# Attention and two expert layers in one kernel: the second batch's keys and values loaded earlier, split with GpSimd, and the dispatch table cleared later

## The chip, the cores and the metric

The kernel runs on one core of a Trainium2 chip. The metric is device time in microseconds (us) of one execution; the runs before the change have a median of 566.87 us (3 runs, 565.37 to 568.51).

## The reference, cut to what matters

```python
# attention: batch 2, heads 8, sequence 576, head size 64
scores = q @ k.T / sqrt(64)
scores = where(scores >= max(scores) - tau, scores, -1e9)
x = (softmax(scores) @ v)                # as 1152 tokens x 512
# dense layer, 512 -> 2048 -> 512
x = elu(x @ w_in) @ w_out
# 8 experts, each token to one of them, at most 288 tokens an expert
e = argmax(x @ w_gate); p = softmax(x @ w_gate)[e]
disp[e, position of the token in e] = x  # slots that no token takes stay zero
out[token] = p * (relu(disp[e] @ w1[e]) @ w2[e])[position]
```

## The kernel before, in words

All matrix work is done in fp16 pairs: a float is split into a high half (the float, scaled and rounded) and a low half (what the rounding left), and three products of halves are summed. A split costs ScalarE the high half and a second engine the low half: VectorE with one instruction on the unscaled float, or GpSimd with a subtraction, for which ScalarE first scales the float in place. `split` (L101) has both forms, "dve" and "pool".

**Steps.** The attention loop (L903) runs 36 steps and two more for what lags. A step i is one tile of 128 query rows (i // 4) and one pair of heads (i % 4). Tiles 0 to 3 belong to the first batch, tile 4 to both, tiles 5 to 8 to the second, so the second batch's keys are first read for step 16's scores, which are issued at the end of step 15, and its values two steps after the scores. One step does, in order:

- PE: the product of probabilities and values of step i - 2 (`emit_pv`, L308);
- SyncE: loads of keys, values and queries (L198 to L211) into `kraw` and `qraw`, which share a ring of two buffers, and `vraw`, with two of its own;
- the splits of keys and values: the first half of each (`prep_k`, `prep_v`, L213 and L224: generators that stop after ScalarE's part);
- VectorE's row maximum (L274), ScalarE's exp (L284) for two heads;
- the second halves of the splits, on VectorE (L219, L229);
- in steps 0 to 16 a conversion of dense-layer weights (`conv`, L363; two a step from step 2 on): three VectorE instructions into one PSUM bank (L369 to L373), two on ScalarE that read it (L380, L381), one on GpSimd (L382), and the load of the weights four conversions ahead (`cst`);
- VectorE's mask (L290), and PE's scores of step i + 1 (L255), which take the PSUM that the mask has read;
- the split of the probabilities (L299 on ScalarE, L300 on GpSimd) and their DMA transpose on SyncE's queue (`pt`, L305);
- from step 7 on chunks of the dense layer, 48 matmuls of the first half (`mma`, L397) or 12 of the second (`mmb`, L429), with their own work on ScalarE (L411, L412, L418), VectorE (L414) and GpSimd (L419);
- every fourth step the attention output (L335 to L346) and the query split (`prep_q`, L234).

Each engine takes its instructions in the order in which the code writes them; SyncE's queue issues DMAs in that order too, and one that waits holds up those behind it. The loop's tables `CONV` and `FILL` say how many conversions and chunks a step has.

**The dispatch table.** `disp` in DRAM has 8 x 288 rows of 2,056 bytes (x in two halves, the gate weight and the token's number). `zero_fill` (L177) clears it in six parts at the ends of steps 8 to 13; `zeroed` then lets `route` (L514) write tokens into it by indirect DMA (L509). The experts read slots 0 to 207 of each expert (`load_x`, L650); slots from 196 on are read only where an expert has more than 196 tokens.

Of the kernel before, what the change touches and what calls it, by code (L numbers as in the profile page):

```python
# [7 lines left out]
F16 = mybir.dt.float16  # L8
# [33 lines left out]
def kernel(  # L42
# [126 lines left out]
    def setup_rest():  # L169
        nc.scalar.activation(out=wg[:, 0], in_=wg_f, func=ACTF.Copy, scale=SC)  # L170
        nc.vector.scalar_tensor_tensor(
            out=wg[:, 1], in0=wg_f, scalar=SC, in1=wg[:, 0], op0=ALU.mult, op1=ALU.subtract
        )
        nc.vector.tensor_copy(ev, ev_i)
        nc.vector.tensor_scalar(ids, ids, OOB_ID, None, ALU.bitwise_xor)

    def zero_fill(part, parts):  # L177
        n = E * CS // P
        r0, r1 = part * n // parts, (part + 1) * n // parts
        if r0 < r1:  # L180
            nc.sync.dma_start(
                out=disp.rearrange("(p r) (a c) -> p (r a) c", p=P, a=2)[:, 2 * r0:2 * r1],
                in_=zero.bitcast(U16).unsqueeze(1).to_broadcast([P, 2 * (r1 - r0), ROW // 2]),
            )
# [27 lines left out]

    def prep_k(b, j):  # L213
        k2 = raw_t.pop(("k", b, j))
        kt = attn.tile([P, 2, S], F16, name="kst", tag="kst", bufs=6)
        flat = kt.rearrange("p h s -> p (h s)")
        nc.scalar.activation(out=flat[0:D], in_=k2, func=ACTF.Copy, scale=SC)
        yield
        nc.vector.scalar_tensor_tensor(  # L219
            out=flat[D:P], in0=k2, scalar=SC, in1=flat[0:D], op0=ALU.mult, op1=ALU.subtract  # L220
        )
        kst[b, j] = kt

    def prep_v(b, j):  # L224
        v1 = raw_t.pop(("v", b, j))
        vt = attn.tile([P, 2, VC], F16, name="vst", tag="vst", bufs=6)
        nc.scalar.activation(out=vt[:, 0], in_=v1, func=ACTF.Copy, scale=SC)
        yield
        nc.vector.scalar_tensor_tensor(  # L229
            out=vt[:, 1], in0=v1, scalar=SC, in1=vt[:, 0], op0=ALU.mult, op1=ALU.subtract  # L230
        )
        vst[b, j] = vt

# [651 lines left out]
    with tc.manual_schedule():  # L885
        setup_first()
        setup_pool()
        for c in "kqgkcvcvcc":
# [8 lines left out]
            else:  # L897
                load_conv(len(stage_t))
        for _ in prep_k(0, 0):
            pass  # L900
        prep_q(0)
        sc = [emit_s(0, z) for z in range(2)]
        for i in range(NSTEP + LAG):  # L903
# [13 lines left out]
            halves = []  # L917
            for b, base in ((0, 0), (1, 4 * NPAIR)):
                jk = i + 1 - base
                if 0 <= jk + 1 < NPAIR and (b or jk >= 1):  # L920
                    load_k(b, jk + 1)
                if 0 <= jk < NPAIR:
                    halves.append(prep_k(b, jk))
                jv = i - base
                if 0 <= jv < NPAIR:
                    halves.append(prep_v(b, jv))
                if 0 <= jv + 1 < NPAIR and (b or jv >= 1):
                    load_v(b, jv + 1)
            if on and j == 0 and t_ + 1 < NTILE:
# [219 lines left out]
```

## Time and profile before

| | us |
|---|---|
| runs before: median, lowest, highest | 566.87, 565.37, 568.51 |
| profiled execution, its own time | 572.67 |
| its span, first to last instruction | 570.6 |
| busy: PE, DVE (VectorE), ACT (ScalarE), POOL (GpSimd) | 438.8, 400.1, 351.1, 266.8 |
| bytes moved by DMA | 105.59 MB, mean 185 GB/s |

The profile is of one execution, taken by the hardware profiler. Busy shares are means over a program with very different stages: attention with the dense layer between its steps (its last step begins at 326 us), the rest of the dense layer and the routing, then the experts. A row that says what an instruction waited for names the one that came last.

### The profile page before, as it was taken

What the parts mean: (1) busy time and instruction counts of PE and PEld (TensorE: products, weight loads), DVE (VectorE), ACT (ScalarE), POOL (GpSimd) and SP (SyncE); (2) the same over time, 40 slices, a digit from 0 to 9 for tenths busy, and PEclk for the clock granted to TensorE, in tenths of its full rate; (3) what the DMA queues carried; (4) which work ended last, traced back from release to release, by engine and by line L of the source; (5) the groups of instructions that cost most, each with busy time, mean ns of one, the idle gap of its engine ahead of it and who ended that gap; (6) DMA issues with size and microseconds to landing.
All of it is one profiled execution on the core that took longest, in us unless ns stands there. A gap on an engine that the chain in (4) does not pass through costs nothing.

```text
span 570.6 us, 13138 instructions
## 1 busy us (share of the span) xinstructions
PE 438.8 (77%) x5343; PEld 360.5 (63%) x5343; DVE 400.1 (70%) x840; ACT 351.1 (62%) x511; POOL 266.8 (47%) x195
## 2 busy tenths in 40 slices
PE   1143439575628889999999999998899997887792
PEld 0032327264506667777777777778799997887771
DVE  4888999998539879888887945765355676646620
ACT  3556577687437875865676756664386665756421
POOL 1236566767505544846656634232442442443232
PEclk9975668978868999999999999997899999799797
DMA  5864988999995556657976765755388989797521
GB/s 165 249 175 116 260 186 232 239 251 255 221 254 138 122 108 141 121 125 113 260 169 86 129 113 187 262 218 186 59 233 254 291 225 259 241 283 201 172 61 40
DMA packets 154227, 105.59 MB, mean 185 GB/s; under 512 B 135209, under 2 KB 142121, under 8 KB 150064
## 3 DMA queue, kind: packets, MB, share of 16 engines
q1 hardware_dynamic: 151520, 99.94, 70.9%
q0 software_dynamic: 2640, 4.74, 2.4%
q8 instruction: 44, 0.72, 0.5%
q14 instruction: 23, 0.19, 0.1%
HBM read 60.06 MB, written 12.68 MB: 127 GB/s over the span
## 4 chain that ended last, share of the span: by engine, by line
PE 26%; DMA 26%; DVE 25%; ACT 10%; issue 9%; POOL 2%; SPq 1%; POOLq 0%; DVEq 0%; ACTq 0%
PE mma L397 9%; DMA stg<-in_w_dram 9%; PE mmb L429 6%; DMA out_dram<-y,ix 5%; DMA kraw<-in_kt_dram 4%; DVE pp L290 4%; PE s L255 3%; DVE we L645 3%; ACT we L642 3%; DVE cvp L370 3%; PE pv L322 3%; DVE m L274 3%; DMA yr<-yt 3%; DVE cvp L369 3%; PE mm L682 2%
## 5 line engine op out<-in xcount | busy, mean ns | idle before, releaser
L255 PE MATMUL s<-kst,qst 128*128 128x288 f16 (+1 forms) x320 | 54.8, 338 | 82.4 <-DVE pp L290 72.6
L300 POOL TENSOR_TENSOR phl<-pp,phl 128x1152 f16<-128x1152 f32 x36 | 85.4, 2373 | 63.1 <-issue 45.1
L397 PEld LDWEIGHTS <-wi 128*128 128x128 f16 x1728 | 103.1, 100 | 4.5 <-issue 1.5
L645 DVE SCALAR_TENSOR_TENSOR we<-stg,we 128x1024 f16<-128x1024 f32 x64 | 79.2, 1274 | 37.2 <-ACT we L642 37.0
L255 PEld LDWEIGHTS <-qst 128*128 128x128 f16 (+1 forms) x320 | 30.3, 114 | 104.4 <-DVE pp L290 50.7
L642 ACT ACTIVATE we<-stg 128x1024 f16<-128x1024 f32 x64 | 64.3, 1047 | 44.0 <-DMA stg<-in_w_dram 43.3
L429 PE MATMUL mmb<-wo,g 128*128 128x512 f16 x384 | 89.7, 382 | 1.9 <-POOL g L419 1.8
L397 PE MATMUL mma<-xt,wi 128*128 128x128 f16 x1392 | 87.0, 225 | 0.5 <-DVE gf L414 0.5
L682 PE MATMUL mm<-xs,we 128*128 128x196 f16 x768 | 72.9, 259 | 13.4 <-DVE we L645 4.6
L682 PEld LDWEIGHTS <-we 128*128 128x128 f16 x768 | 69.4, 103 | 15.9 <-DVE we L645 9.6
L284 ACT ACTIVATE pp<-s,nb,escale 128x576 f32<-128x576 f32 x72 | 58.4, 827 | 24.7 <-DVE nb L275 10.4
L695 POOL TENSOR_TENSOR ht<-rf,ht 128x392 f16<-128x392 f32 x32 | 35.1, 1106 | 77.0 <-ACT ht L694 39.2
L429 PEld LDWEIGHTS <-g 128*128 128x128 f16 x384 | 35.4, 98 | 41.1 <-POOL g L419 3.4
L419 POOL TENSOR_TENSOR g<-gf,g 128x512 f16<-128x512 f32 x36 | 45.3, 1259 | 34.3 <-ACT g L418 34.3
L738 PE MATMUL mm<-ht,we 128*128 128x196 f16 x672 | 57.9, 247 | 1.5 <-DVE yt L749 1.5
L738 PEld LDWEIGHTS <-we 128*128 128x128 f16 x672 | 56.9, 97 | 1.6 <-issue 1.6
L290 DVE SCALAR_TENSOR_TENSOR pp<-s,th,pp 128x576 f32<-128x576 f32 x72 | 55.8, 812 | 2.1 <-ACT pp L284 1.9
L322 PE MATMUL pv<-vst,pt 128*128 128x64 f16 (+3 forms) x1080 | 46.0, 206 | 14.2 <-DMA pt<-phl 12.4
L274 DVE TENSOR_REDUCE m<-s 128x1 f32<-128x576 f32 x72 | 53.8, 748 | 2.1 <-PE s L255 2.1
L322 PEld LDWEIGHTS <-pt 128*128 128x128 f16 (+1 forms) x1080 | 43.6, 107 | 17.2 <-DMA pt<-phl 14.0
L299 ACT ACTIVATE phl<-pp 128x1152 f16<-128x1152 f32 x36 | 41.6, 1156 | 9.5 <-DVE pp L290 9.4
L382 POOL TENSOR_TENSOR wi<-cv,wi 128x512 f16<-128x512 f32 x16 | 18.5, 1155 | 46.5 <-ACT cv L381 46.5
(128 smaller groups left out, 619.5 us busy)
## 6 DMA issues: line engine op xcount, KB each, us to landing
stg<-in_w_dram SPq DMA_DIRECT2D x32, 1024.0 KB, 5.5
cst<-in_w_in_dram SPq DMA_DIRECT2D x16, 512.0 KB, 7.0
cst<-in_w_out_dram SPq DMA_DIRECT2D x16, 512.0 KB, 4.7
disp<-zero SPq DMA_DIRECT2D x6, 771.0 KB, 8.0
qraw<-in_qt_dram SPq DMA_DIRECT2D x9, 512.0 KB, 4.7
vraw<-in_vb_dram SPq DMA_DIRECT2D x8, 320.0 KB, 4.2
kraw<-in_kt_dram SPq DMA_DIRECT2D x8, 288.0 KB, 5.5
out_dram<-zero SPq DMA_DIRECT2D x1, 2304.0 KB, 9.2
```

Source lines behind the costliest of these rows:

```text
L255: nc.tensor.matmul(s[a:z, half, 0:288], q2[:, pas, h, a:z], kst[b, h // 2][:, h % 2, half * 288:(half + 1) * 288], start=(pas == 0), stop= ...
L274: nc.vector.tensor_reduce(out=m, in_=s, axis=AX.XY, op=ALU.max)
L284: nc.scalar.activation(out=pp[:, z].rearrange("p (a c) -> p a c", a=2), in_=s, func=ACTF.Exp, bias=nb, scale=escale,)
L290: nc.vector.scalar_tensor_tensor(out=e, in0=s, scalar=th, in1=e, op0=ALU.is_ge, op1=ALU.mult, accum_out=rsum[t_][:, h:h + 1],)
L300: nc.gpsimd.tensor_tensor(out=d[:, 1], in0=flat, in1=d[:, 0], op=ALU.subtract)
L322: nc.tensor.matmul(o[a:e, h:h + w // D, :].rearrange("p h d -> p (h d)"), q[:, ph * 9 + blk, a:e], vt[:, vh, c:c + w], start=(blk == 4 and ...
L397: nc.tensor.matmul(ps[:, o * P:(o + 1) * P], w[:, wh, kk, :], xt[t_][:, xh * 4 + kk, :], start=(k_ == 0), stop=(k_ == 11),)
L429: nc.tensor.matmul(ps, gt[t_, q][:, gh, o, :], w[:, wh, :], start=(first and o == 0 and n == 0), stop=(last_ and o == QF - 1 and n == 2),)
L642: nc.scalar.activation(out=w[:, 0, part], in_=t[:, part], func=ACTF.Copy, scale=SC)
L645: nc.vector.scalar_tensor_tensor(out=w[:, 1, part], in0=t[:, part], scalar=SC, in1=w[:, 0, part], op0=ALU.mult, op1=ALU.subtract)
L682: nc.tensor.matmul(ps[:, o * n:(o + 1) * n], w[:, wh, kk % 2, f * P:(f + 1) * P], t[:, xh * 4 + kk, :], start=(k_ == 0), stop=(k_ == 11),)
L738: nc.tensor.matmul(ps[:, o * n:(o + 1) * n], w[:, wh, f % 4, j * P:(j + 1) * P], h2[:, gh, f, :], start=(f == 0 and n_ == 0), stop=(f == 7 ...
```

## The change: what it does

- The loads and splits of keys and values follow four tables by step. For the second batch the four key loads move from steps 14 to 17 to steps 9, 11, 14 and 15, their splits from steps 15 to 18 to steps 12, 13, 16 and 17; the value loads from steps 15 to 18 to 12, 13, 16 and 18, their splits from steps 16 to 19 to 14, 15, 19 and 20. The first batch keeps its steps.
- Each split but the very first one of keys takes the form "pool": ScalarE scales in place and copies, GpSimd subtracts. `setup_rest` does the same with the gate weights `wg`.
- The clearing moves to steps 16 to 19, two experts a step, and covers slots 0 to 207 of each expert alone; in step 20 one small DMA clears the last 8 bytes of the rows from slot 208 on.

```diff
@@ -67,7 +67,12 @@
-    ZSTEP, ZPARTS, ZOUT = 8, 6, 26
+    ZIDS, ZSLOTS, ZOUT = 20, 16, 26
+
+    KLOAD = {0: (0, 2), 1: (0, 3), 9: (1, 0), 11: (1, 1), 14: (1, 2), 15: (1, 3)}
+    KPREP = {0: (0, 1), 1: (0, 2), 2: (0, 3), 12: (1, 0), 13: (1, 1), 16: (1, 2), 17: (1, 3)}
+    VLOAD = {1: (0, 2), 2: (0, 3), 12: (1, 0), 13: (1, 1), 16: (1, 2), 18: (1, 3)}
+    VPREP = {0: (0, 0), 1: (0, 1), 2: (0, 2), 3: (0, 3), 14: (1, 0), 15: (1, 1), 19: (1, 2), 20: (1, 3)}
@@ -167,20 +172,26 @@
-        nc.scalar.activation(out=wg[:, 0], in_=wg_f, func=ACTF.Copy, scale=SC)
-        nc.vector.scalar_tensor_tensor(
-            out=wg[:, 1], in0=wg_f, scalar=SC, in1=wg[:, 0], op0=ALU.mult, op1=ALU.subtract
-        )
+        split(wg[:, 0], wg[:, 1], wg_f, SC, "pool")
...
-    def zero_fill(part, parts):
-        n = E * CS // P
-        r0, r1 = part * n // parts, (part + 1) * n // parts
-        if r0 < r1:
+
+    CREAD = min(CS, -(-CMAIN // 16) * 16)
+
+    def zero_slots(e):
+        nc.sync.dma_start(
+            out=disp[e * CS:e * CS + CREAD].rearrange("(p r) (a c) -> p (r a) c", r=2, a=2),
+            in_=zero.bitcast(U16)[0:CREAD // 2].unsqueeze(1).to_broadcast([CREAD // 2, 4, ROW // 2]),
+        )
+
+    def zero_ids():
+
+        for a in range(CREAD, CS, P):
+            m = min(P, CS - a)
             nc.sync.dma_start(
-                out=disp.rearrange("(p r) (a c) -> p (r a) c", p=P, a=2)[:, 2 * r0:2 * r1],
-                in_=zero.bitcast(U16).unsqueeze(1).to_broadcast([P, 2 * (r1 - r0), ROW // 2]),
+                out=disp.rearrange("(e s) c -> s e c", e=E)[a:a + m, :, 2 * DM:],
+                in_=zero.bitcast(U16)[0:m, 0:4].unsqueeze(1).to_broadcast([m, E, 4]),
             )
@@ -210,26 +221,29 @@
-    def prep_k(b, j):
+    def prep(hi, lo, src, where):
+        if where == "pool":
+            nc.scalar.activation(out=src, in_=src, func=ACTF.Copy, scale=SC)
+            nc.scalar.activation(out=hi, in_=src, func=ACTF.Copy)
+            yield
+            nc.gpsimd.tensor_tensor(out=lo, in0=src, in1=hi, op=ALU.subtract)
+        else:
...
+    def prep_k(b, j, where="pool"):
         k2 = raw_t.pop(("k", b, j))
-        kt = attn.tile([P, 2, S], F16, name="kst", tag="kst", bufs=6)
+        kst[b, j] = kt = attn.tile([P, 2, S], F16, name="kst", tag="kst", bufs=6)
         flat = kt.rearrange("p h s -> p (h s)")
...
+        return prep(flat[0:D], flat[D:P], k2, where)
...
@@ -915,17 +929,14 @@
-            for b, base in ((0, 0), (1, 4 * NPAIR)):
-                jk = i + 1 - base
-                if 0 <= jk + 1 < NPAIR and (b or jk >= 1):
-                    load_k(b, jk + 1)
-                if 0 <= jk < NPAIR:
-                    halves.append(prep_k(b, jk))
-                jv = i - base
-                if 0 <= jv < NPAIR:
-                    halves.append(prep_v(b, jv))
-                if 0 <= jv + 1 < NPAIR and (b or jv >= 1):
-                    load_v(b, jv + 1)
+            if i in KPREP:
+                halves.append(prep_k(*KPREP[i]))
+            if i in VPREP:
+                halves.append(prep_v(*VPREP[i]))
+            if i in KLOAD:
+                load_k(*KLOAD[i])
+            if i in VLOAD:
+                load_v(*VLOAD[i])
@@ -965,9 +976,12 @@
-            if ZSTEP <= i < ZSTEP + ZPARTS:
-                zero_fill(i - ZSTEP, ZPARTS)
-                zeroed[0] = i == ZSTEP + ZPARTS - 1
+            if ZSLOTS <= i < ZSLOTS + E // 2:
+                for e in range(2):
+                    zero_slots(2 * (i - ZSLOTS) + e)
+            if i == ZIDS:
+                zero_ids()
+                zeroed[0] = True
```

From the attention code on, the changed kernel's lines stand some 14 higher: its L288 is L274 of before, L298 is L284, L319 is L305, L374 is L360.

How it moves instructions. SyncE's queue before, from the last zero transfer, at the end of step 13, to the transpose of step 15 (L181 is a zero transfer, L200 a key load, L360 a weight load, L305 a transpose of probabilities):

```order
L360 DMA cst<-in_w_out_dram 128x1024
L181 DMA disp<-zero 128x6x514
L200 DMA kraw<-in_kt_dram 64x1152
L360 DMA cst<-in_w_out_dram 128x1024
L305 DMA_TRANSPOSE pt<-phl 128x18x128
L360 DMA cst<-in_w_out_dram 128x1024
L200 DMA kraw<-in_kt_dram 64x1152
L205 DMA vraw<-in_vb_dram 128x640
L305 DMA_TRANSPOSE pt<-phl 128x18x128
```

SyncE's queue in the changed kernel, from the first key load of the second batch in step 9 to the first value load in step 12:

```order
L211 DMA kraw<-in_kt_dram 64x1152
L374 DMA cst<-in_w_out_dram 128x1024
L319 DMA_TRANSPOSE pt<-phl 128x18x128
L360 DMA_TRANSPOSE xt<-xhl 128x8x128
L374 DMA cst<-in_w_out_dram 128x1024 x2
L319 DMA_TRANSPOSE pt<-phl 128x18x128
L374 DMA cst<-in_w_out_dram 128x1024
L211 DMA kraw<-in_kt_dram 64x1152
L374 DMA cst<-in_w_in_dram 128x1024
L319 DMA_TRANSPOSE pt<-phl 128x18x128
L374 DMA cst<-in_w_in_dram 128x1024
L216 DMA vraw<-in_vb_dram 128x640
```

The first key load stands ahead of step 9's transpose and no zero transfer is among these rows; before, it stands one transpose ahead of its split, behind the last zero transfer. The zero transfers of the changed kernel follow the transposes of steps 16 to 19 (L183; L532 and L360 are transposes of the routing and of the attention output):

```order
L319 DMA_TRANSPOSE pt<-phl 128x18x128
L183 DMA disp<-zero 416x1x514 x2
L319 DMA_TRANSPOSE pt<-phl 128x18x128
L360 DMA_TRANSPOSE xt<-xhl 128x8x128
L532 DMA_TRANSPOSE x2t<-x_2216 128x8x128
L183 DMA disp<-zero 416x1x514 x2
L216 DMA vraw<-in_vb_dram 128x640
L319 DMA_TRANSPOSE pt<-phl 128x18x128
L183 DMA disp<-zero 416x1x514 x2
L319 DMA_TRANSPOSE pt<-phl 128x18x128
```

ScalarE in step 12 before, from the last conversion of step 11 to the first of step 12:

```order
L381 ACTIVATE cv<-cvp 128x512
L299 ACTIVATE phl<-pp 128x1152
L380 ACTIVATE wo_1259<-cvp 128x512
L381 ACTIVATE cv<-cvp 128x512
L284 ACTIVATE pp<-s,nb,escale 128x576 x2
L411 ACTIVATE ef<-mma 128x512
L412 ACTIVATE ef<-ef,lnsc 128x512
L380 ACTIVATE wo_1370<-cvp 128x512
L381 ACTIVATE cv<-cvp 128x512
```

and in the changed kernel:

```order
L394 ACTIVATE wo_1268<-cvp 128x512
L395 ACTIVATE cv<-cvp 128x512
L226 ACTIVATE kraw<-kraw 64x1152
L227 ACTIVATE kst<-kraw 64x1152
L298 ACTIVATE pp<-s,nb,escale 128x576 x2
L425 ACTIVATE ef<-mma 128x512
L426 ACTIVATE ef<-ef,lnsc 128x512
L394 ACTIVATE wo_1384<-cvp 128x512
L395 ACTIVATE cv<-cvp 128x512
```

The two halves of the key split (L226 in place, L227) stand between the conversion and the exps. VectorE in step 0 before, from the last threshold to the first mask:

```order
L280 TENSOR_SCALAR th<-m,cadd 128x1 x2
L219 SCALAR_TENSOR_TENSOR kst<-kraw,kst 64x1152
L229 SCALAR_TENSOR_TENSOR vst<-vraw,vst 128x640
L369 TENSOR_SCALAR cvp<-cst 128x512
L370 SCALAR_TENSOR_TENSOR cvp<-cst,cvp 128x512
L373 SCALAR_TENSOR_TENSOR cvp<-cst,cvp 128x512
L290 SCALAR_TENSOR_TENSOR pp,rsum<-s,th,pp 128x576 x2
```

and in the changed kernel, where the conversion follows the threshold at once:

```order
L294 TENSOR_SCALAR th<-m,cadd 128x1 x2
L383 TENSOR_SCALAR cvp<-cst 128x512
L384 SCALAR_TENSOR_TENSOR cvp<-cst,cvp 128x512
L387 SCALAR_TENSOR_TENSOR cvp<-cst,cvp 128x512
L304 SCALAR_TENSOR_TENSOR pp,rsum<-s,th,pp 128x576 x2
```

## Rows read from the trace of the kernel before

**Rows 1.** The page: the chain that ended last, share of the span by engine.

```profile
PE 26%; DMA 26%; DVE 25%; ACT 10%; issue 9%; POOL 2%; SPq 1%; POOLq 0%; DVEq 0%; ACTq 0%
```

**Rows 2.** Busy us by stage: length, PE, PEld, DVE, ACT, POOL, clock, DMA share, GB/s.

```profile
10.35:54.55 44.20, 12.81 (x100) 8.62 (x99) 37.32 (x68) 24.28 (x32) 15.62 (x10) 0.78 0.71 203
54.55:87.20 32.65, 14.36 (x140) 10.42 (x138) 31.67 (x68) 21.95 (x31) 21.92 (x15) 0.66 0.83 209
87.20:120.45 33.25, 22.51 (x263) 15.63 (x261) 32.27 (x70) 25.78 (x38) 24.03 (x17) 0.91 1.04 240
120.45:138.70 18.25, 13.62 (x182) 12.13 (x180) 17.41 (x38) 13.74 (x21) 12.22 (x9) 0.81 1.09 235
138.70:150.27 11.57, 7.47 (x77) 5.15 (x75) 8.32 (x19) 7.22 (x12) 6.92 (x6) 0.85 1.03 283
150.27:173.95 23.68, 9.92 (x118) 7.39 (x117) 9.50 (x18) 9.53 (x13) 6.48 (x5) 0.74 1.02 207
173.95:185.49 11.54, 9.48 (x130) 7.25 (x128) 11.17 (x21) 8.16 (x12) 5.77 (x5) 0.95 0.62 152
185.49:196.59 11.10, 9.40 (x141) 6.80 (x139) 9.58 (x20) 8.87 (x13) 6.23 (x5) 1.00 0.49 111
196.59:215.69 19.10, 17.37 (x264) 12.76 (x262) 15.12 (x28) 13.24 (x18) 10.64 (x7) 1.00 0.53 108
215.69:246.11 30.42, 30.42 (x440) 23.77 (x438) 26.94 (x72) 21.43 (x30) 19.45 (x12) 1.00 0.61 124
```

**Rows 3.** Chain of waits, step 15: start, length (us), what.

```profile
155.90 9.25 DMA kraw<-in_kt_dram
165.17 1.17 ACT kst L217
166.37 1.35 DVE kst L219
```

**Rows 4.** Waits: ScalarE from 138 to 175 us, then PE from 84 to 203.

```profile
ACT kst L217 <- DMA kraw<-in_kt_dram: 12.4, 1, 12.4
...
PE pv L322 <- DMA pt<-phl: 11.6, 4, 4.6
```

**Rows 5.** Timeline of SyncE's queue, steps 13 to 15: start, length (us), instruction.

```profile
144.32 8.64 SPq L305 DMA_TRANSPOSE pt<-phl  x1
...
155.90 0.54 SPq L200 DMA_DIRECT2D kraw<-in_kt_dram  x1
...
175.10 2.74 SPq L305 DMA_TRANSPOSE pt<-phl  x1
```

**Rows 6.** Instructions by line and shape: count, busy (us), mean ns, idle before.

```profile
L300 POOL TENSOR_TENSOR phl<-pp,phl 128x1152 f16<-128x1152 f32 x36 | 85.4, 2373 | 63.1 <-issue 45.1 <-PE s L255 5.0 <-ACT phl L299 3.7
L219 DVE SCALAR_TENSOR_TENSOR kst<-kraw,kst 64x1152 f16<-64x1152 f32 x8 | 12.8, 1596 | 18.0 <-ACT kst L217 17.7
L229 DVE SCALAR_TENSOR_TENSOR vst<-vraw,vst 128x640 f16<-128x640 f32 x8 | 9.4, 1174 | 5.8 <-ACT vst L227 5.7
L217 ACT ACTIVATE kst<-kraw 64x1152 f16<-64x1152 f32 x8 | 9.3, 1158 | 21.4 <-DMA kraw<-in_kt_dram 21.4
L227 ACT ACTIVATE vst<-vraw 128x640 f16<-128x640 f32 x8 | 5.8, 728 | 2.7 <-DMA vraw<-in_vb_dram 1.8 <-PE pv L322 0.8
```

**Rows 7.** Timeline, steps 1 to 3: start, length (us), engine, instruction, idle before.

```profile
22.27 1.16 ACT L217 ACTIVATE kst<-kraw 64x1152 f16<-64x1152 f32 x1 [1.04 <-DMA kraw<-in_kt_dram]
...
30.62 2.34 DVE L171 SCALAR_TENSOR_TENSOR wg<-wg_f,wg 128x32 f16<-128x32 f32 x1 [1.35 <-ACT wg L170]
...
46.82 2.22 DVE L229 SCALAR_TENSOR_TENSOR vst<-vraw,vst 128x640 f16<-128x640 f32 x1 [1.75 <-ACT vst L227]
```

**Rows 8.** The page, DMA issues: count, KB each, median us to landing.

```profile
disp<-zero SPq DMA_DIRECT2D x6, 771.0 KB, 8.0
```

**Rows 9.** Timeline of PE, one chunk of 48 matmuls in steps 12 and 17.

```profile
119.85 4.79 PE L397 MATMUL mma<-xt,wi 128*128 128x128 f16 x48
...
193.06 2.85 PE L397 MATMUL mma<-xt,wi 128*128 128x128 f16 x48
```

More of the change, by code (lines that the diff above doesn't have):

```diff
@@ L211, in load_q, with prep_v @@
         raw_t["q", t_] = t
-    def prep_k(b, j):
+    def prep(hi, lo, src, where):
[5 more added lines that the diff above has]
+        else:
+            nc.scalar.activation(out=hi, in_=src, func=ACTF.Copy, scale=SC)
+            yield
+            nc.vector.scalar_tensor_tensor(
+                out=lo, in0=src, scalar=SC, in1=hi, op0=ALU.mult, op1=ALU.subtract
+            )
+    def prep_k(b, j, where="pool"):
         k2 = raw_t.pop(("k", b, j))
-        kt = attn.tile([P, 2, S], F16, name="kst", tag="kst", bufs=6)
+        kst[b, j] = kt = attn.tile([P, 2, S], F16, name="kst", tag="kst", bufs=6)
         flat = kt.rearrange("p h s -> p (h s)")
[L217 to L224, printed above, removed]
-        v1 = raw_t.pop(("v", b, j))
[L226 to L232, printed above, removed]
+        return prep(flat[0:D], flat[D:P], k2, where)
+    def prep_v(b, j, where="pool"):
+        v1 = raw_t.pop(("v", b, j))
+        vst[b, j] = vt = attn.tile([P, 2, VC], F16, name="vst", tag="vst", bufs=6)
+        return prep(vt[:, 0], vt[:, 1], v1, where)
     def prep_q(t_):
@@ L898 @@
                 load_conv(len(stage_t))
-        for _ in prep_k(0, 0):
+        for _ in prep_k(0, 0, "dve"):
             pass
```

## The prediction, as put on record

> **What bounds the kernel now.** I read the page first, then the busy time by stage, then the chain of waits where a stage is longer than its busiest engine, and last the queue of SyncE there. The page gives the whole: the chain that ended last is split almost evenly between PE, DMA and DVE [rows 1], so no engine bounds the whole span, and the stages have to be read one by one. Stage edges are the starts of the first L274 of a step; step 0 begins at 10.35 us, the last of the 36 at 326.
>
> In [rows 2] the reader is to see four regimes. Steps 0 to 3 take 44.20 us, and steps 4 to 7 take 32.65 us at 31.67 us of DVE: DVE is the bound there, and a step costs 8.16 us. Steps 8 to 11 are the same with zero transfers beside them (33.25 us, DVE 32.27, DMA share 1.04). So the zero transfers cost nothing there, though the DMA engines are full. Then step 14 takes 11.57, step 15 takes 23.68 with no engine busy for even 10 us, steps 16 and 17 take 11.54 and 11.10 us. From step 20 on PE is busy without a gap (30.42 of 30.42 us for four steps).
>
> The 23.68 us are explained by the chain: a load of keys issued at 155.90 takes 9.25 us, and ScalarE's split of it starts at 165.17 [rows 3]. ScalarE waits 12.4 us for it, with both exps of the step queued behind; PE waits 11.6 us in four places for transposed probabilities, 4.6 at the longest [rows 4]. Why both are late stands in SyncE's queue [rows 5]: one pt transpose holds it for 8.64 us from 144.32, and the key load is issued behind it, behind a zero transfer, one step ahead of its use. With the last zero transfer landed, a pt transpose holds the queue 2.74 us.
>
> **Steps 14 to 17: the main term.** The change issues the second batch's first keys in step 9 and splits them in step 12, with no zero transfer in steps 8 to 13. The wait of 12.4 us goes, and so does the late cst that stretched step 14. What is late next is ScalarE: each split there becomes two ACTIVATEs and stands ahead of the exps. A split of keys costs it 2 × 1.158 = 2.3 us, one of values 2 × 0.728 = 1.5 us [rows 6]. From ScalarE's busy time of the same steps [rows 2], with the old splits out and the new pairs in: step 14: 7.22 + 1.5 = 8.7; step 15: 9.53 − 1.2 + 1.5 = 9.8; step 16: 8.16 − 1.2 − 0.7 + 2.3 = 8.6; step 17: 8.87 − 1.2 − 0.7 + 2.3 = 9.3; together 36.4 us, which is over the 8.2 us of a DVE-bound step. VectorE loses 1.596 and 1.174 us a split, so it is no longer the bound. In steps 15 and 16 I add 1.9 us for the second conversion, whose PSUM bank frees only after ScalarE has read the first one: 38.3. Before: 11.57 + 23.68 + 11.54 + 11.10 = 57.9. **Gain 19.6 us**; the ends are 13.9 (four steps of 11, as steps 16 and 17 are now) and 24.6 (four of 8.3).
>
> **Steps 12 and 13** get a key split each, which they did not have: ScalarE 13.74 + 2 × 2.3 = 18.4 of the 18.25 us that they take. I add 1.4 us; ends 0 (it all fits into ScalarE's waits) and 4.6 (both pairs on the path).
>
> **Steps 0 to 3.** VectorE loses three key splits and four value splits and the split of wg, which alone takes 2.34 us at 30.62 for 32 elements a partition, as long as the GpSimd subtraction beside it; the value split at 46.82 takes 2.22 against a mean of 1.174 [rows 6, 7]. Step by step, with the order of the changed kernel: in step 0 the exps start 0.7 us later (a second pass over the values), but the conversion no longer stands behind two splits, so the mask comes 1.4 us earlier. In step 1 the keys land at 22.27 as now [rows 7]; two pairs put the exps 1.9 us later, the mask still 1.0 earlier, and the 2.34 us of wg go: 4.4 gained so far. In step 2 the load of the next keys waits for GpSimd's subtraction, 0.4 us later than now, and two pairs cost 0.6 us more: 3.4. In step 3 VectorE's 2.22 us go: **gain 5.6 us**. Ends: 9 (all the VectorE time removed but waits for data) and −2 (the pairs, 3 × 1.158 + 4 × 0.728 = 6.4 us of ScalarE, mostly on the path).
>
> **Steps 18 and 19** lose two waits of ScalarE in front of the exps, for the slot of old values; PE is busy 17.37 of 19.10 us [rows 2]: **gain 1.7**, ends 0 and 4.
>
> **GpSimd** gets 7 key and 8 value subtractions: 2.373 us for 1,152 elements [rows 6], values about 1.4 (an estimate, by length from the same row), one a step from step 12 on. In steps 12 to 17 its busy time is 5.8 to 6.9 us a step now [rows 2], so it comes to 7.9 to 8.6 of the 9.7 us that I give these steps: nearly full, but behind it wait only pt (used two steps later) and the conversions' weights. I cost it at nothing beyond ScalarE; if that cover is gone, it is rival 1. Two loads that reuse a raw slot now wait for GpSimd; behind them on SyncE stand only cst loads and a pt whose subtraction comes after it on GpSimd anyway: nothing. wg on GpSimd: nothing, first read in step 20.
>
> **The zero transfers** move to steps 16 to 19: eight of 418 KB, 3.3 MB, where 4.6 MB were. A pair of 835 KB, priced by the row of 771 KB in 8.0 us [rows 8], drains in 8.7 us, about a step; the DMA share of these steps is 0.49 to 0.62 now, and they lose half of the key and value loads. PE-bound steps begin there, and pt is what they can wait for. I take 2 us lost; ends 0 (nothing waited in steps 8 to 11 under a share of 1.04) and 18 (four waits of 4.6 [rows 4]). The ids transfer is small: nothing. Dispatch by tokens starts after step 20 in both programs, so the later clearing holds nothing. From step 20 to the end the order on PE is the same row by row.
>
> **Sum:** 19.6 − 1.4 + 5.6 + 1.7 − 2.0 = 23.5 us. The profiled execution took 572.67 us with a span of 570.6, so it would take 549.2; it lies 5.8 us over the median of 566.87, and against that median the forecast is 543.4, said as **543 us**.
>
> **Rivals.** *1: ScalarE and GpSimd become the bound.* For: the splits' second pass stands ahead of the exps, and GpSimd is nearly full in steps 12 to 17. Against: both have waits in these steps. With the low ends of steps 12 to 17 and 2 us left of the gain in steps 0 to 3: 13.9 − 4.6 + 2.0 + 1.7 − 2.0 = 11 us gained, **556 us**. [...]
>
> *2: the stall moves instead of going, and the kernel is slower.* The zero pairs back up in steps 16 to 19, the last two value loads and the query loads land as late as the keys do now, and ScalarE stands in front of the exps twice for 12.4 us, with PE waiting twice 4.6 us for pt: 34 us lost against 25.5 gained (the sum without the 2.0), **575 us**. It decides from where a pair takes much longer than a step of 8.6 us to drain; by the row it takes 8.7. Against: the value loads stand 2 and 3 steps ahead of their use, the cst loads are over by then. [...]
>
> [...]
>
> *4: the loads go but their place does not matter,* since the 15 us of step 15 belong to this execution, 5.8 us over the median: then the main term is smaller by about those 5.8, **549 us**; this lies within my forecast's range.
>
> **How the numbers follow.** Forecast with its spread (531 to 550): 0.66. Rival 1: 0.19. Rival 2: 0.04. Rival 3: 0.05. The high ends of steps 0 to 3 and 14 to 17 together, under 531: 0.06. The range leaves out rivals 2 and 3 and a part of the last: 530 to 557. About 0.5% (2.8 us) is what a measurement of this kernel can tell from no change. Faster: the forecast, rival 1, the case under 531 and a fifth of rival 3, whose 564 lies on the edge: 0.92; the rest of rival 3 is no change, 0.04; rival 2 is slower, 0.04.
>
> **What would show it.** Right: step 15 (first L288 to first L288 in the new lines) near 10 us with no wait of ScalarE for kraw; pt transposes near 2.7 us on SyncE in steps 8 to 15; step 4 beginning near 49 us; VectorE without splits after the first; PE full from about step 17 on. Wrong: ScalarE waiting for vraw in steps 19 and 20, pt waits on PE over 4 us in steps 18 to 22, or steps 12 to 17 above 10.5 us each with ScalarE or GpSimd busy throughout.

## The result and the profile after

The changed kernel takes **544.17 us** (median of 4 runs, 542.38 to 548.67) where the kernel before, run beside it, takes 567.69 us (4 runs, 565.37 to 574.34): a ratio of 0.9582, 95% interval 0.9531 to 0.9632. The forecast was 543 us. The profiled execution took 542.38 us with a span of 540.7.

The first view is again the busy time by stage, cut at the start of the first L288 of a step (L274 before; nearly all lines moved by 14). Columns: stretch, length, then PE, PEld, DVE, ACT and POOL busy (count of instructions), granted clock, DMA share, GB/s. The rows are steps 0 to 3, 12 and 13 together, 14, 15, 16, 17, 18 and 19 together, 20 to 23; they answer to [rows 2].

```profile
10.32:47.47 37.15, 13.15 (x104) 9.01 (x103) 27.17 (x60) 29.99 (x40) 28.44 (x18) 1.00 0.84 242
113.42:132.65 19.23, 14.84 (x192) 13.23 (x190) 17.65 (x39) 17.46 (x25) 16.02 (x10) 0.77 1.09 274
132.65:141.00 8.35, 8.34 (x106) 6.35 (x105) 8.13 (x18) 7.64 (x12) 7.41 (x7) 0.94 1.03 197
141.00:151.40 10.40, 8.02 (x111) 5.63 (x109) 8.34 (x19) 10.14 (x15) 9.19 (x7) 1.00 0.89 224
151.40:160.58 9.18, 7.65 (x106) 5.45 (x104) 8.32 (x18) 8.48 (x12) 8.04 (x6) 1.00 0.66 154
160.58:173.62 13.04, 10.67 (x170) 7.84 (x168) 9.19 (x18) 8.65 (x12) 10.79 (x7) 1.00 0.67 148
173.62:189.43 15.81, 14.64 (x205) 10.85 (x203) 11.10 (x26) 13.93 (x19) 9.82 (x6) 1.00 1.00 187
189.43:220.99 31.56, 31.08 (x450) 24.17 (x448) 27.03 (x72) 21.66 (x30) 20.81 (x13) 1.00 0.89 160
```

Step 15 went from 23.68 to 10.40 us, with ScalarE busy for 10.14 of them. Steps 0 to 3 went from 44.20 to 37.15. Step 17 is longer, 13.04 for 11.10, and steps 18 and 19 shorter, 15.81 for 19.10. The largest waits of ScalarE from step 14 to step 21 (what waited, for what, us in total, times, longest) name no load of keys or values, nor does any smaller one, in the place of the 12.4 us of [rows 4]:

```profile
ACT xhl L357 <- DVE xf L352: 3.5, 2, 3.0
ACT pp L298 <- DVE nb L289: 2.8, 2, 2.3
ACT pp L298 <- POOL g L433: 2.4, 2, 1.7
```

SyncE's queue in steps 17 to 21 (start, length, instruction) shows what the clearing does in its new place, in the manner of [rows 5]. Each pair of clearing transfers is followed, after other entries, by the pt transpose of the step:

```profile
164.88 2.05 SPq L183 DMA_DIRECT2D disp<-zero  x2
170.29 2.78 SPq L319 DMA_TRANSPOSE pt<-phl  x1
...
176.46 1.82 SPq L183 DMA_DIRECT2D disp<-zero  x2
...
181.24 4.05 SPq L319 DMA_TRANSPOSE pt<-phl  x1
185.34 1.82 SPq L183 DMA_DIRECT2D disp<-zero  x2
188.98 5.25 SPq L319 DMA_TRANSPOSE pt<-phl  x1
...
195.65 1.82 SPq L183 DMA_DIRECT2D disp<-zero  x2
...
199.35 5.43 SPq L319 DMA_TRANSPOSE pt<-phl  x1
```

From a pair's issue to the end of that transpose it is 8.2, 8.8, 8.9 and 9.1 us (188.98 + 5.25 − 185.34 = 8.9). The pair itself is done sooner: in the trace's records of single packets (zeros go in packets of 1,028 bytes) the last one of a pair ends 6.3, 6.8, 8.4 and 7.4 us after the issue. PE waits for pt once from step 19 to step 23, for 0.5 us:

```profile
PE pv L336 <- DMA pt<-phl: 0.5, 1, 0.5
```

From the start of step 0 to that of step 35 it was 315.69 us and is 291.34: 24.35 us gained. Another 5.6 us lie behind that (244.57 and 239.01 us from the start of step 35 to the end), in a part that the change does not touch; the section on the prediction comes back to them.

### The profile page after: what moved, and what is told of

Same layout as the page of the kernel before. It is cut to its first block, busy times and chain, and to the rows that moved or that the text cites. A ratio compares the mean times of both kernels' runs of the same rounds, so it can differ in the third digit from the quotient of the medians.

```text
span 540.7 us, 13169 instructions
## 1 busy us (share of the span) xinstructions
PE 433.3 (80%) x5343; PEld 356.8 (66%) x5343; DVE 382.9 (71%) x824; ACT 362.7 (67%) x527; POOL 295.9 (55%) x211
## 5 line engine op out<-in xcount | busy, mean ns | idle before, releaser
L659 DVE SCALAR_TENSOR_TENSOR we<-stg,we 128x1024 f16<-128x1024 f32 x64 | 80.4, 1291 | 36.5 <-ACT we L656 36.3
L696 PE MATMUL mm<-xs,we 128*128 128x196 f16 x768 | 71.0, 256 | 12.3 <-DVE we L659 4.5
L696 PEld LDWEIGHTS <-we 128*128 128x128 f16 x768 | 68.0, 101 | 14.4 <-DVE we L659 8.4
L709 POOL TENSOR_TENSOR ht<-rf,ht 128x392 f16<-128x392 f32 x32 | 36.5, 1150 | 73.8 <-issue 35.3
L298 ACT ACTIVATE pp<-s,nb,escale 128x576 f32<-128x576 f32 x72 | 58.0, 826 | 24.6 <-DVE nb L289 18.3
L752 PE MATMUL mm<-ht,we 128*128 128x196 f16 x672 | 57.9, 247 | 1.0 <-DVE yt L763 1.0
L752 PEld LDWEIGHTS <-we 128*128 128x128 f16 x672 | 56.9, 97 | 1.1 <-issue 1.1
L288 DVE TENSOR_REDUCE m<-s 128x1 f32<-128x576 f32 x72 | 53.9, 749 | 1.8 <-PE s L269 1.8
L336 PE MATMUL pv<-vst,pt 128*128 128x64 f16 (+3 forms) x1080 | 44.9, 204 | 4.5 <-DVE xf L352 2.9
L790 POOL DMA_INDIRECT out_dram<-y,ix x16 | 23.8, 1487 | 18.6 <-ACT y L780 13.6
```

What stands on the lines that cost most here:

```text
L288: nc.vector.tensor_reduce(out=m, in_=s, axis=AX.XY, op=ALU.max)
L298: nc.scalar.activation(out=pp[:, z].rearrange("p (a c) -> p a c", a=2), in_=s, func=ACTF.Exp, bias=nb, scale=escale,)
L336: nc.tensor.matmul(o[a:e, h:h + w // D, :].rearrange("p h d -> p (h d)"), q[:, ph * 9 + blk, a:e], vt[:, vh, c:c + w], start=(blk == 4 and ...
L659: nc.vector.scalar_tensor_tensor(out=w[:, 1, part], in0=t[:, part], scalar=SC, in1=w[:, 0, part], op0=ALU.mult, op1=ALU.subtract)
L696: nc.tensor.matmul(ps[:, o * n:(o + 1) * n], w[:, wh, kk % 2, f * P:(f + 1) * P], t[:, xh * 4 + kk, :], start=(k_ == 0), stop=(k_ == 11),)
L752: nc.tensor.matmul(ps[:, o * n:(o + 1) * n], w[:, wh, f % 4, j * P:(j + 1) * P], h2[:, gh, f, :], start=(f == 0 and n_ == 0), stop=(f == 7 ...
```

## The experiments

Theory: step 15 stood because its keys were issued one step ahead into a queue full of zero transfers, so both the place of the loads and the clearing count; GpSimd's part is the time in steps 0 to 3. Rivals: the clearing made the stall alone; the early loads are the whole of it; VectorE's splits bound steps 12 to 17.

**One part of the change at a time.** Four kernels. The kernel before with the new clearing alone (`c_clear_only`):

```diff
-            if ZSTEP <= i < ZSTEP + ZPARTS:
-                zero_fill(i - ZSTEP, ZPARTS)
+            if ZSLOTS <= i < ZSLOTS + E // 2:
+                for e in range(2):
+                    zero_slots(2 * (i - ZSLOTS) + e)
```

> The kernel before with only the clearing changed: slots read in full are cleared in steps 16 to 19, ids in step 20; loads stay one step ahead and second halves on VectorE. Theory (the stall of step 15 needs both the late issue and the full queues): without zero transfers a pt transpose holds SyncE 2.7 us in steps 14 and 15 and the key load takes about 5 us where it took 9.25, but it is still issued one step ahead, so step 15 goes from 23.7 to about 15 and 2 us go to the zeros in 16 to 19: about 560 us, ratio 0.988. Rival (the zero transfers alone made the stall): step 15 near 10 us and nearly the whole main term, 551 to 554 us, ratio near 0.975. Rival (the clearing moves the stall to the value loads, now issued one step ahead amid the zeros): step 17 to 19 longer by 10 or more, 567 us or over.

The new tables of loads and splits alone, every second half on VectorE, old clearing (`a_early_only`; as a diff against the changed kernel):

```diff
-    def prep_k(b, j, where="pool"):
+    def prep_k(b, j, where="dve"):
-    def prep_v(b, j, where="pool"):
+    def prep_v(b, j, where="dve"):
-        split(wg[:, 0], wg[:, 1], wg_f, SC, "pool")
+        split(wg[:, 0], wg[:, 1], wg_f, SC, "dve")
```

> The kernel before with only the second batch's loads and splits earlier; second halves stay on VectorE, zero transfers in steps 8 to 13 over all slots as before. Theory: ScalarE's wait of 12.4 us for keys goes, late pt transposes and weight loads under the zeros stay, so step 15 is about 13 and steps 14 to 17 about 46 where they were 58: about 556 us, ratio 0.98. Rival (the zero transfers alone made the stall): the loads sit in the same full queues and the exps wait for them in step 12 or 13 instead, 565 us, ratio 0.995 or over. Rival (the early place is the whole of it): steps 14 to 17 at 41 as in the changed kernel, 551 us, ratio 0.97.

The second halves on GpSimd alone, in the old steps (`b_pool_only`: the new `prep` and `split(..., "pool")` in the kernel before):

> The kernel before with only the second halves of keys, values and gate weights on GpSimd. Theory: steps 0 to 3 gain the 7 us that they gained in the changed kernel, step 15 stays near 23 us since its keys come as late as before: 560 us, ratio 0.987. Rival (VectorE's splits are part of what bounds steps 14 to 17): another 4 to 5 us there, 555 us, ratio 0.98. Rival (two passes on ScalarE before the exps cost as much as VectorE saves): 567 us, ratio 1.0.

And loads and GpSimd together with the old clearing (`ab_no_clear`: the changed kernel with `zero_fill` in steps 8 to 13):

> The changed kernel with the old clearing: all slots, six transfers in steps 8 to 13. Theory (both the place of the loads and the clearing count): 549 to 552 us, ratio 0.972, with pt transposes of 4 to 8 us on SyncE and weight loads late in steps 13 to 15. Rival (the loads' place is all, the clearing is free anywhere): 543 to 545 us, as the changed kernel. Rival (the clearing made the stall): 560 us, step 15 near 20.

Lengths in us, from the starts of a step's first maximum in each profile, and the runs:

| stage | before | changed | clearing alone | loads alone | GpSimd alone | loads and GpSimd |
|---|---|---|---|---|---|---|
| steps 0 to 3 | 44.20 | 37.14 | 43.41 | 43.56 | 38.35 | 36.73 |
| 12 and 13 | 18.24 | 19.23 | 17.85 | 22.89 | 17.86 | 20.71 |
| 14 and 15 | 35.25 | 18.75 | 21.15 | 25.68 | 33.97 | 26.35 |
| 16 and 17 | 22.63 | 22.22 | 22.63 | 21.95 | 24.99 | 24.25 |
| 18 and 19 | 19.10 | 15.81 | 21.97 | 15.09 | 17.36 | 15.80 |
| 20 to 34 | 110.36 | 112.23 | 110.58 | 112.74 | 111.37 | 111.73 |
| gained from 0 to 34 | | 24.35 | 11.8 | 7.9 | 5.9 | 14.0 |
| median, us | 567.7 | 544.2 | 560.9 | 563.1 | 561.0 | 555.7 |
| ratio | | 0.958 | 0.988 | 0.992 | 0.990 | 0.979 |
| 95% interval | | 0.953 to 0.963 | 0.983 to 0.993 | 0.988 to 0.996 | 0.983 to 0.996 | 0.975 to 0.983 |

Clearing alone and GpSimd alone came within 1 us of their theories' 560; the loads alone took 563.1 us for 556 expected, and loads with GpSimd 555.7 for 549 to 552: the old clearing costs more than I had given it. Up to step 34 the three parts add up nearly: 11.8 + 7.9 + 5.9 = 25.6 against 24.35. By the medians they are 6.8, 4.6 and 6.7 us, together 18.0 against 23.5, from runs of each kernel that spread over 4 to 8 us; so the shares rest on the profiles, one execution of each kernel. By these the largest is the **clearing**, not the loads. With it alone the keys are still issued one step ahead, and step 15 falls from 23.69 to 12.90; ScalarE's waits there name no load any more (kernel with the clearing alone, steps 13 to 16):

```profile
ACT wo L389 <- DVE cvp L382: 6.1, 5, 2.0
ACT wi L389 <- DVE cvp L382: 2.7, 4, 1.4
```

With GpSimd alone the same wait stands as it was, in step 15:

```profile
ACT kraw L212 <- DMA kraw<-in_kt_dram: 11.9, 1, 11.9
```

The loads alone shorten steps 14 and 15 by 9.6 and pay 4.65 of it back in steps 12 and 13: under the zero transfers PE waits for pt instead (kernel with the loads alone, steps 12 to 16):

```profile
PE pv L327 <- DMA pt<-phl: 19.0, 5, 6.2
```

So a rival was right for step 15 itself: taking the zero transfers out of steps 8 to 13 is enough to bring its keys in time. The early loads are needed where the clearing now stands: with the clearing alone steps 18 and 19 take 21.97 us for 19.10, since keys and values issued one step ahead are late there, as that experiment's last rival had it, though for less (the same kernel, these two steps):

```profile
ACT vst L236 <- DMA vraw<-in_vb_dram: 4.7, 2, 4.5
ACT kst L226 <- DMA kraw<-in_kt_dram: 2.1, 1, 2.1
```

**Place or sum of the clearing?** `z8_trimmed` is the changed kernel with one number changed, `ZSLOTS = 8` for 16: the same eight smaller transfers, in steps 8 to 11.

> The changed kernel with its eight smaller clearing transfers (two a step, slots read in full alone) put back to steps 8 to 11. Theory (zeros beside the weight loads of steps 8 to 13 make SyncE's queue late, whatever their sum): pt transposes of 6 to 8 us in steps 9 to 13, steps 12 to 15 at about 45 us where the changed kernel has 38, 2 us back in steps 18 to 28: 549 to 552 us. Rival (3.3 MB for 4.6 is what helped, not the place): 542 to 545 us.

555.65 us (ratio 0.9804, 0.9741 to 0.9868): 11.5 us worse than the changed kernel, though it clears no more, and the same as with the old clearing of 4.6 MB (555.7), so the smaller sum gains nothing there. Steps 8 to 11, where the pairs now are, take 33.26 us, no more than without them (33.28); but steps 12 to 15 take 45.87 us where they took 37.98. The pairs and the pt behind them take 9.9 to 12.9 us, and steps 12 to 15 stand for weights and for pt:

```profile
PE pv L336 <- DMA pt<-phl: 15.6, 3, 7.1
DVE cvp L383 <- DMA cst<-in_w_in_dram: 7.2, 3, 3.6
ACT kraw L226 <- DMA kraw<-in_kt_dram: 3.1, 1, 3.1
```

So the place counts: by these waits the weight loads (cst), two a step up to step 16, and the zeros do not both fit there. `clear_spread` goes the other way, one transfer a step in steps 16 to 23:

```diff
-            if ZSLOTS <= i < ZSLOTS + E // 2:
-                for e in range(2):
-                    zero_slots(2 * (i - ZSLOTS) + e)
+            if ZSLOTS <= i < ZSLOTS + E:
+                zero_slots(i - ZSLOTS)
```

> The changed kernel with one clearing transfer a step in steps 16 to 23 instead of two a step in 16 to 19, the ids after the last. Theory (two transfers a step are what holds pt in steps 18 to 20): pt transposes near 3 us there, the 2 us lost in steps 20 to 34 halve: 543 us. Rival (the loss in steps 20 to 34 has nothing to do with the clearing): 544 us, steps 21, 22 and 28 as in the changed kernel. Rival (tokens can be dispatched only from step 24 on, and the experts wait): 547 us or over, the time after step 34 longer by 3.

548.39 us (0.9668, 0.9609 to 0.9726). The pt transposes of steps 18 to 20 are short, 2.7 to 3.7 us, as the theory had it, but those of 22 to 24 now take 4.5 to 5.3, the first tokens are dispatched at 235.11 us for 212.71, and steps 20 to 27 take 63.98 us for 60.79. A single wait for pt of 3.65 us is among it, in step 26.

**What GpSimd is worth in the second batch.** `b1_dve` gives the second batch's second halves back to VectorE:

```diff
-                halves.append(prep_k(*KPREP[i]))
+                halves.append(prep_k(*KPREP[i], ["pool", "dve"][KPREP[i][0]]))
...
-                halves.append(prep_v(*VPREP[i]))
+                halves.append(prep_v(*VPREP[i], ["pool", "dve"][VPREP[i][0]]))
```

> The changed kernel with the second batch's second halves on VectorE by one instruction, and one pass of ScalarE ahead of the exps; the first batch's stay on GpSimd. Theory (ScalarE's second pass and VectorE's split cost about the same in steps 12 to 20): 543 to 546 us, steps 12 to 20 within 2 us of the changed kernel. Rival (the second pass on ScalarE bounds steps 12 to 17): 3 to 5 us less there, 540 us. Rival (VectorE bounds them): 5 to 8 us more, 550 us.

556.68 us (0.9816, 0.9769 to 0.9864), 12.5 us over the changed kernel, where the worst rival had 8. Two things make it up. Steps 12 to 15 take 43.47 us for 37.98, with VectorE busy almost throughout (here steps 12 and 13):

```profile
114.88:125.07 10.19, 7.64 (x115) 6.97 (x113) 9.82 (x20) 7.59 (x11) 5.15 (x4) 0.89 0.97 271
125.07:137.11 12.04, 6.27 (x77) 5.42 (x75) 11.54 (x23) 8.16 (x12) 7.00 (x6) 0.74 0.74 212
```

Steps 16 to 19 then give 1.7 back, and steps 20 to 27 lose 8.0. The pair of the clearing issued at 193.76 leaves SyncE with its pt 8.8 us later, as in the changed kernel; but steps 17 to 20, under which the four pairs run, are shorter here (31.78 us for 36.54), so the queue has less time for the same transfers and PE asks sooner (SyncE's queue, the chain of waits, then PE):

```profile
193.76 1.82 SPq L183 DMA_DIRECT2D disp<-zero  x2
195.70 6.85 SPq L319 DMA_TRANSPOSE pt<-phl  x1
```

```profile
195.70 10.63 DMA pt<-phl
```

```profile
206.38 1.94 PE L336 MATMUL pv<-vst,pt 128*64 128x128 f16 x54 [2.31 <-DMA pt<-phl]
208.25 2.76 PE L443 MATMUL mmb<-wo,g 128*128 128x512 f16 x12
...
218.43 1.04 PE L336 MATMUL pv<-vst,pt 128*128 128x128 f16 x27 [3.71 <-DVE x L521]
219.30 4.44 PE L443 MATMUL mmb<-wo,g 128*128 128x512 f16 x12
```

The second wait is put down to a small copy of VectorE (L521), which ended at that moment. The pt that this product reads was issued at 208.67, behind the fourth pair, and in `scale_dve` below PE's waits in the same steps all name pt (us in total, times, longest), so it was probably pt here too:

```profile
PE pv L336 <- DMA pt<-phl: 6.4, 3, 3.6
```

After the second wait the same twelve matmuls take 4.44 us instead of 2.76, at a granted clock of 0.87 in that step. The changed kernel has the same queue and waits 0.5 us: it passes close by.

**By whom the transfers are issued.** `b1_dve_actq` is that kernel with `nc.scalar.dma_start` for `nc.sync.dma_start` in `zero_slots`.

> The kernel with the second batch's halves on VectorE (556.7 us), its eight clearing transfers issued by ScalarE instead of SyncE. Theory (the 9 us that it lost in steps 20 to 27 are pt transposes held in SyncE's queue behind a pair of transfers): pt transposes of steps 18 to 20 near 3 us on SyncE, steps 20 to 27 near 61 us, 549 us. Rival (the DMA engines are full and it does not matter by whom the transfers are issued): pt still lands late, 556 us. Rival (ScalarE is held by the issues and the exps wait): 560 us or over.

557.36 us (0.9794, 0.9721 to 0.9866), no better. The transposes hold SyncE as long as before, with the pair now in ScalarE's queue:

```profile
178.61 7.24 SPq L319 DMA_TRANSPOSE pt<-phl  x1
...
209.29 5.78 SPq L319 DMA_TRANSPOSE pt<-phl  x1
```

So my reading that they stand *behind* the pair in SyncE's queue fell: they are slow beside it, whoever issues it. Of the 8 us of steps 20 to 27, four came back (64.91 for 68.80), and steps 18 and 19 lost five.

**From how many partitions the zeros are read.** Three kernels change the layout of the source alone (`clear_16p` shown; `clear_13p` has 13 for 16; `clear_96p` clears 192 of 208 slots by 96 partitions, and the rest in step 20):

```diff
-            out=disp[e * CS:e * CS + CREAD].rearrange("(p r) (a c) -> p (r a) c", r=2, a=2),
-            in_=zero.bitcast(U16)[0:CREAD // 2].unsqueeze(1).to_broadcast([CREAD // 2, 4, ROW // 2]),
+            out=disp[e * CS:e * CS + CREAD].rearrange("(p r) (a c) -> p (r a) c", p=16, a=2),
+            in_=zero.bitcast(U16)[0:16].unsqueeze(1).to_broadcast([16, CREAD // 8, ROW // 2]),
```

> The changed kernel with each clearing transfer read from 16 partitions of the zero tile (each repeated 26 times) instead of 104 (4 times); the same bytes to the same places. [...] Rival (the place counts, not the layout): the same 544 us, pt transposes as now. Rival (few source partitions are read more slowly): pt transposes over 6 us, 546 us or over.

> The changed kernel with each clearing transfer read from 13 partitions of the zero tile (each repeated 32 times) instead of 104. In the kernel that read from 16 partitions a pair of transfers and the pt transpose behind it ended 13.0, 12.2 and 15.0 us after the pair's issue, where the changed kernel has 8.9. Theory (few source partitions are read slowly): 13 us or more from a pair's issue to the end of the pt behind it, steps 20 to 27 at 79 us or over, 566 us or over. [...]

> The changed kernel with 192 of an expert's 208 slots cleared from 96 partitions (which 16 divides) in steps 16 to 19, the other 16 slots of all experts by two transfers of 16 partitions in step 20. Theory (few source partitions are read slowly, many are not): about 8.5 us from a pair's issue to the end of the pt behind it, steps 16 to 20 as in the changed kernel; the two last transfers may hold the pt of step 21 by 6 us, 546 us. [...]

| source partitions | 104 (changed) | 16 | 13 | 96 |
|---|---|---|---|---|
| pair's issue to end of the pt behind it, mean of 4, us | 8.8 | 13.1 | 14.8 | 8.2 |
| one zero packet, median, ns | 47 | 153 | 152 | 47 |
| zero packets in flight, mean | 9.9 | 13.5 | 10.5 | 12.8 |
| first to last packet of a pair, mean of 4, us | 5.65 | 9.59 | 11.53 | 4.14 |
| steps 20 to 27, us | 60.79 | 79.42 | 89.23 | 60.28 |
| median, us | 544.17 | 566.32 | 573.97 | 547.06 |
| ratio to before | 0.958 | 0.999 (0.995 to 1.003) | 1.012 (1.008 to 1.016) | 0.964 (0.958 to 0.971) |

With few partitions the zeros drain slower than the steps run, and everything behind them is late: with 16, ScalarE waits once for the last values and PE for pt; with 13 the more (ScalarE and PE of each, steps 19 to 22):

```profile
ACT vraw L226 <- DMA vraw<-in_vb_dram: 5.7, 1, 5.7
...
PE pv L336 <- DMA pt<-phl: 15.2, 3, 6.8
```

```profile
ACT vraw L226 <- DMA vraw<-in_vb_dram: 9.6, 1, 9.6
...
PE pv L336 <- DMA pt<-phl: 21.6, 3, 8.9
```

That is rival 2 of the prediction, brought about by the layout. The single packets (832 in a pair, 768 with 96 partitions) show two effects. Read from 13 or 16 partitions a packet takes over three times as long (152 and 153 ns for 47); that is the slow reading of the theory. And more packets are in flight (begun and not yet ended) with 16 and 96 partitions (13.5 and 12.8 on average) than with 13 and 104 (10.5 and 9.9), so that 16 partitions are quicker than 13 (9.59 us for a pair, and 11.53), and 96 partitions move 0.92 of the bytes in 0.73 of the time. Little of this second effect reaches the kernel: from a pair's issue to the end of its pt it is 8.2 us for 8.8, part of which is the transpose's wait for GpSimd, and steps 20 to 27 take 60.28 us for 60.79. With 96 partitions steps 0 to 34 take 291.7 us, the changed kernel's 291.3; the 3 us between the medians lie behind step 34.

**ScalarE's second pass.** `scale_dve` lets VectorE scale the raw values, so that ScalarE makes one pass and GpSimd still subtracts:

```diff
-            nc.scalar.activation(out=src, in_=src, func=ACTF.Copy, scale=SC)
-            nc.scalar.activation(out=hi, in_=src, func=ACTF.Copy)
+            nc.scalar.activation(out=hi, in_=src, func=ACTF.Copy, scale=SC)
             yield
+            nc.vector.tensor_scalar(src, src, SC, None, ALU.mult)
```

> The changed kernel with ScalarE making the first half in one pass again; the scaling of the raw values, which was its first pass (1.157 us of keys, 0.723 of values), goes to VectorE behind the maxima of the step, and GpSimd subtracts as now. Theory (ScalarE's second pass stands on the path in steps 0 to 3 and 15 to 17, where VectorE waits 7.7 us in four places and 2.1 us for exps): steps 0 to 3 at 34 to 35 us where the changed kernel has 37.1 to 38.5, steps 14 to 17 at 39 where it has 41.0, 540 us. Rival (VectorE's new work takes as much as ScalarE gives up, stretched where GpSimd works beside it): 544 us, all steps within 0.7 us. Rival (VectorE becomes the bound again, as in the kernel with the second batch's halves there): steps 12 to 17 longer by 5, 549 us or over.

552.16 us (0.9715, 0.9674 to 0.9755): worse by 8. The scaling takes VectorE about as long as a split would (1.17 us of values and 1.60 of keys in the kernel before [rows 6]; here count, busy us, mean ns, idle before):

```profile
L228 DVE TENSOR_SCALAR vraw<-vraw 128x640 f32<-128x640 f32 x8 | 9.2, 1156 | 5.7 <-ACT vst L226 3.9 <-issue 1.8
L228 DVE TENSOR_SCALAR kraw<-kraw 64x1152 f32<-64x1152 f32 x7 | 9.0, 1287 | 2.5 <-ACT kst L226 1.8 <-POOL g L433 0.4
```

Steps 12 to 15 take 42.24 us (37.98 in the changed kernel), steps 16 and 17 gain 2.5, and steps 20 to 27 lose 8.3, as in `b1_dve` (steps 17 to 20 take 32.60 us here). Steps 0 to 3, for which the theory had 34 to 35 us, take 40.12. None of the variants is faster than the changed kernel.

## Why the prediction was right, and where not

**The sum** was 23.5 us, and steps 0 to 34 gained 24.35. That it is so close is in part luck: 2.7 us less than said in steps 14 to 17 stand against 3.1 more in steps 0 to 3 and 18 and 19, and of the 2.0 us given to the zeros most was lost to something else. The terms one by one:

- *Steps 14 to 17, gain 19.6:* 16.9 (57.9 to 41.0), inside the ends. Steps 14, 15 and 16 came near the lengths worked out from ScalarE (8.36, 10.39, 9.19 for 8.7, 10.8, 9.5), though ScalarE was full in step 15 alone (10.14 of 10.40 us); in step 14 it was busy for 7.64 of 8.35 us and PE for 8.34. **Step 17 failed:** 13.03 for 9.3. The sum counted ScalarE's busy time alone. In the step ScalarE's pair of 2.3 us stands ahead of the exps, and then a tiny operation of VectorE takes 2.29 us, while GpSimd's subtraction runs from 167.88 to 170.26:

```profile
168.00 2.29 DVE L349 TENSOR_SCALAR rinv<-rsum,eps,xsc 128x8 f32<-128x8 f32 x1
170.32 0.20 DVE L350 RECIPROCAL rinv<-rinv 128x8 f32<-128x8 f32 x1
170.56 0.69 DVE L352 TENSOR_TENSOR xf<-pv,rinv 128x512 f32<-128x512 f32 x1
```

  L349's median is 0.28 us. It ends with GpSimd's instruction (at 170.29 us, that one at 170.26), and ScalarE waits 3.0 us for what follows. What ties the two was not shown beyond these times. The other kernels with the new steps agree on its cost: where this operation takes 0.87 us (`ab_no_clear`) step 17 takes 11.54, and where it takes 0.28 (`a_early_only`, `b1_dve`, `b1_dve_actq`, `scale_dve`) 9.6 to 11.0. So some 2.0 of the 3.7 us too many are this; the rest was not taken apart.
- *Why the term was as large as it was* I had half wrong. The text let the wait for keys go for two causes in one sentence, the issue in step 9 and no zero transfer in steps 8 to 13, and gave them one price. It read from steps 8 to 11 that the zeros cost nothing there, which is so (33.25 us with them, 33.28 without), and set no price of their own for the steps behind. The clearing alone also ends that wait, and the loads alone, under the old clearing, turn half of their gain into waits for pt. In the old place the clearing cost some 10 to 12 us (11.8 alone, 24.35 − 14.0 = 10.3 on top of the rest), nearly all of it behind step 11.
- *Steps 12 and 13, loss 1.4:* 1.0. *Steps 18 and 19, gain 1.7:* 3.3; with step 17, which grew, 1.4 (30.20 to 28.84).
- *Steps 0 to 3, gain 5.6:* 7.1 in this profile; with GpSimd alone 5.9, and 5.6 to 7.5 over all kernels with the same first steps. The split of wg takes GpSimd 0.244 us, for 2.34 on VectorE [rows 7]:

```profile
L110 POOL TENSOR_TENSOR wg<-wg_f,wg 128x32 f16<-128x32 f32 x1 | 0.2, 244 | 0.0
```

- *The zeros in 16 to 19, loss 2.0:* about 0.5. Steps 20 to 27 took 60.79 us, and 60.32 with no zeros there (`ab_no_clear`). A pair, priced at 8.7 us by the row of 771 KB, was drained 6.3 to 8.4 us after its issue. That price was too high: the transfers of 771 KB took 8.0 us to land, but moved their packets in 4.1 (from the first to the last, mean of 6). Of the zero packets 13 were most often in flight in the changed kernel and 16 with 96 partitions, and for the same bytes 96 partitions take 0.79 of the time.
- *From step 20 on, nothing:* steps 20 to 34 take 1.9 us more (110.36 to 112.23), 0.5 with the zeros and 1.1 in step 28, of which the next term tells.
- *GpSimd at nothing:* no other engine waits long for its new work (VectorE twice, 0.8 us together), but beside it small operations of VectorE become long, as in step 17 and again in step 28, in its 8.69 us:

```profile
255.73 2.14 DVE L509 SCALAR_TENSOR_TENSOR slot_f<-pos,slot_f,over 128x1 f32<-128x1 f32 x1
```

  GpSimd splits probabilities from 255.47 to 257.85. In every kernel in which this operation takes 2.1 us in step 28 the step takes 8.7, and 7.6 or 7.7 in those where it takes 0.22. On the other side, the value of having GpSimd was under-told. Without it in the second batch the kernel takes 12.5 us more: 5.5 in steps 12 to 15, where VectorE is the bound, and 8.0 in steps 20 to 27 by waits for pt and the slower PE behind them, which no term of mine had.
- *The signs:* step 15 without a wait for keys came, and step 4 began at 47.47 us for 49. The transposes of steps 8 to 15 held SyncE for 2.7 to 4.1 us, not near 2.7 throughout, and PE was full from step 20 on, not from 17 (10.67 of 13.04 us).

**The rivals.** *1* (ScalarE and GpSimd the bound) fell. ScalarE is nearly full in step 15, but giving its second pass to VectorE made the kernel slower. GpSimd takes longer for 1,152 elements, 2.37 us [rows 6] for VectorE's 1.35 [rows 3], but here VectorE was the bound, and by the runs the work is better off on GpSimd (544.17 us, and 556.68 with the second batch's on VectorE). *2* fell for this kernel and is real. It decides by the drain time of a pair, as said: from a pair's issue to the end of its pt it is 8.8 us here and 13.1 with 16 partitions, and between the two lies the whole gain. *3*, the 564 us among the chances, stood for a PE at a lower granted clock in steps 14 to 19, and fell: no run shows that loss, and the clock is 0.94 in step 14 and 1.00 from step 15 to 23. *4* was right that part of the difference belongs to the profiled execution of before, and wrong on the place: step 15 is 23.3 us also in the kernel with GpSimd alone. It is most likely behind step 34, as the steps before it repeat from kernel to kernel where nothing was changed. That part takes 244.57 us in the profile of before and 237.5 to 245.9 in the profiles of the other kernels, also between kernels that differ only in the clearing (239.0 and 245.9). What makes it vary was not tried; the granted clock there differs from profile to profile (mean 0.94 before, 0.96 in the changed kernel).

## What to carry to other kernels

A load that lands late may be late because of what else fills the DMA engines (here step 15 fell from 23.69 to 12.90 us with the zeros alone moved): look at bulk transfers without a due time first, and put them where the next compulsory loads have ended, and where steps are longer than the transfers take to drain. Moving work off a full VectorE paid here even at nearly twice the duration (2.37 us for 1.35), where the new engine's result was used steps later; look then for small VectorE operations that fall beside GpSimd's on the way to PE (2.29 us for 0.28 in step 17). A kernel whose PE just meets its transposes can lose 8 us when the steps that carry the bulk transfers become 4 to 5 us shorter, as two of the variants did, so read the wait that is nearly there, too.

## What the runs showed of the hardware

- Zeros broadcast from 13 or 16 partitions took 14.8 and 13.1 us for a pair of 835 KB with the transpose behind it, from 104 partitions 8.8: a packet of 1,028 bytes took 152 and 153 ns there and 47 here, which I had not weighed at all. Why so few partitions are read slowly was not shown. The two have nearly the same time for one packet; what sets them apart is the number in flight, 10.5 and 13.5 on average.
- A DMA transpose is slowed by a bulk transfer beside it also when another engine issues that transfer (it holds SyncE for 7.24 us with the pair in ScalarE's queue, for 2.7 with none).
- A VectorE operation on 8 elements a partition took 2.29 us beside a GpSimd subtraction (0.28 alone), one on a single element 2.14 (0.22); scaling 640 elements took 1.16 us on average.
